# Norms of one group made in parts, and fetches asked for piece by piece, in a chunked delta rule with a maxout FFN behind it

## The chip, the cores and the metric

The kernel runs on one core of a Trainium2 chip. The core has five engines, each with a queue of its own that it works off in order: PE (TensorE, matmuls and transposes into PSUM), DVE (VectorE), ACT (ScalarE), POOL (GpSimd) and SP (SyncE, which here only issues DMAs). POOL and ACT issue DMAs too. The metric is the device time of one execution in microseconds, as the median of several runs.

## The reference

A delta rule over 4 batches x 8 heads, 768 tokens, head size 48; its output, 3072 tokens x 384, goes through a feed-forward net whose hidden value is the largest of three products:

```python
k_n = k / (np.linalg.norm(k, axis=-1, keepdims=True) + 1e-06)
for t in range(S):
    y[:, :, t] = einsum('bhd,bhde->bhe', q[:, :, t], state)
    v_old = einsum('bhde,bhd->bhe', state, k_n[:, :, t])
    state = state + beta[:, :, t] * outer(k_n[:, :, t], v[:, :, t] - v_old)
x = y.transpose(0, 2, 1, 3).reshape(B * S, H * D)        # 3072 x 384
h = maximum(maximum(x @ w1, x @ w2), x @ w3)             # 384 -> 768
out = h @ w_out                                          # 768 -> 384
```

q, k, v and beta are fp32. The four weight matrices come as 64-bit floats.

## The kernel before, in words

**The delta rule in chunks.** The 768 tokens are 12 chunks `c` of 64 tokens; two chunks make a group `m` (six groups, 512 tokens each over the four batches). Keys and queries are loaded in units `n` (two to a chunk). For a unit, `turn` (L329) puts keys and queries on the other axis by PE transposes, and `gram` (L411) makes the products of keys with keys and queries. The triangular systems of a whole group are solved on DVE by `solve(m)` (L514), a generator: it makes the key norms (`norm`, L275, one square root on ACT and five small DVE operations), turns them for the values (`norms_of`, L292, four DVE transposes), makes the scale (L539 to L549), scales the matrix once (L560) and then takes 31 elimination steps of two DVE operations each (L574 and L578). Each `yield` ends one part; `some(solving, n)` runs the next n parts.

**The recurrence.** Along the chunks run the links, each a function with a letter: `z` (`join_z`), `j` (`join_u`), `k` (`old_k`: keys times state on PE, L756, subtracted from the values on DVE, L768), `q` (`old_q`), `u` (`new`), `s` (`step`: a product on PE, L807, added to the state by DVE, L814), `y` (`to_y`, the sum on DVE in L828) and `x` (`to_x`, the transpose for the FFN). `e`, `f` and `d` (`halves_z`, `halves_u`, `turn_t1`) finish the solved blocks. Values are scaled with the norms on POOL (`scale`, L302).

**The FFN between which they stand.** `ffn(m)` (L1249) is a generator too: each yield ends one product of 128 hidden rows (`p_h`, L1261), which ACT copies out (L1269) or DVE joins by a maximum (L1275). In group 0 a product covers 256 tokens; a product is six matmul rows of the profile. The loop over `ffn(0)` (L1505) hands out the rest of the work between these pieces `i` by tables: `FIRST` (links of chunk 1, solve parts `S1`, query transposes `T4` to `T7`), `EARLY_LINKS`, `SOLVED` (further solve parts of group 1), `CONVERTED`, `FETCHED`, `LESS`. The schedule is written out by hand (`manual_schedule`): each engine and each DMA queue runs its instructions in the order in which this loop emits them.

**Weights.** There are 24 pieces of 128 x 384 numbers (0 to 17 of the three hidden matrices, 18 to 23 of the output matrix). `fetch` (L220) brings the next piece's 64-bit words into one of five buffers `w_bits` (384 KB). `weights` (L236) makes fp32 of it: three ACT operations (L255 to L257), and one part later, in `join_last`, a shift on DVE (L266) and an add on POOL (L270); `mant` and `up` between them have two buffers each. A buffer is free for the fetch five pieces later when the ACT operations have read it.

**Queues.** `load_q(n)` (L142) issues two DMAs into one of three query buffers and so waits for the transposes of unit n-3. `load_v(c)` (L145) issues two DMAs into one of three value buffers. `queries` (L1486) runs `load_q(n + 3)` behind each `T` n, on SP. Before the change, between the pieces of `ffn(0)`, SP's queue holds: weight 8, queries 4, 5, weight 9, queries 6, weight 10, values 2, weights 11 and 12, queries 7, weight 13, queries 8, 9, 10, values 3 and 4.

The group that the change calls second is `m == 1`. Its `solve` stands at the start of `ffn(0)`: its first part is run before the loop (L1417), then come 10 parts in pieces 0 to 3 (`S1` in `FIRST`) and the rest by `SOLVED`. Its work array `y_p` is one of the three large PSUM buffers (`two`), so that the links have two left until it is done.

Of the kernel before, what the change touches and what calls it, by code (L numbers as in the profile page):

```python
# [23 lines left out]
def kernel(  # L24
# [93 lines left out]
    def rows(bb):  # L118
        return slice(C * bb, C * (bb + 1))
# [6 lines left out]
    def load(src, dst, n, queues):  # L126
        c, g = divmod(n, 2)
        for bb in range(2):
            queues[bb].dma_start(
                out=dst[rows(bb ^ g), :, 0:D],  # L130
                in_=src[2 * bb + g, :, c * C : (c + 1) * C, :].rearrange(
                    "h p d -> p h d"
                ),
            )
# [7 lines left out]
    def load_q(n, queues=one_queue):  # L142
        load(q, qpad[n % NQ], n, queues)

    def load_v(c, queue=nc.sync):  # L145
        vts[c] = work.tile([128, 2, H, D], FP32, name="v_t", bufs=3)
        for bb in range(2):
            queue.dma_start(  # L148
                out=vts[c][rows(bb)].rearrange("p g h d -> p (g h) d"),
                in_=v[2 * bb : 2 * bb + 2, :, c * C : (c + 1) * C, :].rearrange(  # L150
                    "b h p d -> p (b h) d"
                ),
            )
# [132 lines left out]
    def small(name, *shape):  # L286
        one = name[-1] == "0" or name[-2:] == "bl" or name == "warm"
        return work.tile([128, *shape], FP32, name=name, bufs=2 - one)
# [3 lines left out]
    def norms_of(m, bl):  # L292
        for cc in range(2):
            t = small("nrm", 48)
            for bb in range(2):
                at = 16 * (1 - bb)
                nc.vector.transpose(
                    out=t[rows(bb), at : at + BL], in_=bl[rows(cc)]
                )
            nrms[2 * m + cc] = t[:, 16:32].rearrange("p (g h) -> p g h", g=2)  # L300

    def scale(c, nrm):  # L302
        (nc.vector if c > 9 else nc.gpsimd).tensor_tensor(
            out=vts[c], in0=vts[c],
            in1=nrm[:, :, :, None].to_broadcast([128, 2, H, D]), op=ALU.mult,
        )
# [207 lines left out]
    def solve(m):  # L514
# [15 lines left out]
        if m == 1:  # L530
            y = ps_two("y_p").rearrange("p b (j i) -> p (b j) i", i=BL)
            nc.scalar.copy(y, zero.to_broadcast(y.shape))
        if m == 2:
            yield
        if m:
            norms_of(m, bl)
            if m == 2:
                yield
            nc.vector.reciprocal(bl, bl)  # L539
        else:  # L540
            bl_0.append(bl)
            bl = small("inv_bl", BL)
            nc.vector.reciprocal(bl, bl_0[0])
# [11 lines left out]
        else:  # L555
            size, xv, yv = BL, x[:, None], y[:, None]
            xb, by = x, bl[:, None, :].to_broadcast([128, BL, BL])
        if m == 2:
            yield
        nc.vector.tensor_tensor(out=xb, in0=xb, in1=by, op=ALU.mult)  # L560
        yield
        for j in range(size - 1):
            a, b = j + 1, size - 1 - j
            n = BL // size
# [19 lines left out]
        if m == 0:  # L584
# [3 lines left out]
            for i in range(4):  # L588
                if i % 2:
                    n = H * (i == 3)  # L590
# [895 lines left out]
    def queries(names):  # L1486
# [9 lines left out]


    CONVERTED = {*range(6), *range(11, 17), 18, *range(21, 30)}
    FETCHED = {8: 1, 12: 1, 13: 1, 14: 1, 21: 2, 22: 1, 23: 1, 24: 1, 25: 1}
    LESS = {3: 0, 6: 1, 9: 2, 18: 3, 21: 4, 25: 5}  # L1500
    SOLVED = {
        **{i + 4: n for i, n in enumerate((3, 2, 2, 2, 3, 3, 3, 3, 2, 2))},
        27: 1, 28: 1, 29: 1, 30: 6, 31: 17, 32: 6, 33: 5,
    }
    for i, _ in enumerate(ffn(0)):  # L1505
        if i < 7:
            fetch(nc.sync if i else nc.gpsimd)
        if i == 0:
            scale(1, nrm_0[:, 1])
        if i == 1:  # L1510
            load_q(4)
            load_q(5)
        if i == 2:
            load_q(6)
        if i < 6:
            join_last()
        for _ in range(FETCHED.get(i, 0)):
            fetch(nc.gpsimd)
        queries(FIRST.get(i, ""))
        links(1, EARLY_LINKS.get(i, ""))  # L1520
        if i == 26:
            solving = solve(2)
            some(solving, 1)
        if i in CONVERTED:
            some(conv, 1)
        if i == 0:
            fetch(nc.gpsimd)
        some(solving, SOLVED.get(i, 0))
        if i in (8, 13):
            prep_values(i // 4)  # L1530
        if i in (4, 8):
            for n in range(2):
                load_k(8 + 2 * (i > 4) + n, (nc.gpsimd, nc.gpsimd))
        if i == 11:
            load_q(11, (nc.gpsimd, nc.gpsimd))
        if i in (3, 9, 10, 21):
            load_v((3, 9, 10, 21).index(i) + 2)
        if i == 18:
            blocks(2)
        if i == 30:  # L1540
            prep_values(4)
        if i in (29, 30, 31):
            load_blocks(i - 17, nc.sync)
        if i in LESS:
            less_first(LESS[i], nc.gpsimd if i < 10 else nc.vector)
        if i in (30, 31):
            turn_first((2 * i - 60, 2 * i - 59))
        if i == 31:
            turn_first((4, 5))
            for t in range(KT):  # L1550
                both_layers(t)
                if t == 0:
                    links(1, "x1")
# [53 lines left out]
```

## Time and profile before

| | |
|---|---|
| median of 3 runs | 503.69 us (503.05 to 505.37) |
| the profiled execution | 505.88 us |
| its span, first to last instruction | 504.2 us |
| mean granted TensorE clock | 0.969 |
| PE busy | 481.9 us, 96% |
| DVE busy | 354.8 us, 70% |
| ACT busy | 168.7 us, 33% |
| POOL busy | 189.8 us, 38% |
| DMA | 53.51 MB, 106 GB/s over the span |

The shares are means over stages that differ. The start (to some 45 us) is the first group's solve with little for PE to do. From 45 us on the FFN gives PE work between the links; the change lies between 45 and 90 us. From some 105 us to the end PE is hardly ever idle. An engine's row in the order of time gives the start, the length and, in brackets, how long the engine was idle ahead of it and what ended that; "issue" there means that it waited for nothing that the profile shows.

### The profile page before, as it was taken

What the parts mean: (1) busy time and instruction counts of PE and PEld (TensorE: products, weight loads), DVE (VectorE), ACT (ScalarE), POOL (GpSimd) and SP (SyncE); (2) the same over time, 40 slices, a digit from 0 to 9 for tenths busy, and PEclk for the clock granted to TensorE, in tenths of its full rate; (3) what the DMA queues carried; (4) which work ended last, traced back from release to release, by engine and by line L of the source; (5) the groups of instructions that cost most, each with busy time, mean ns of one, the idle gap of its engine ahead of it and who ended that gap; (6) DMA issues with size and microseconds to landing.
All of it is one profiled execution on the core that took longest, in us unless ns stands there. A gap on an engine that the chain in (4) does not pass through costs nothing.

```text
span 504.2 us, 18764 instructions
## 1 busy us (share of the span) xinstructions
PE 481.9 (96%) x8100; PEld 344.5 (68%) x8100; DVE 354.8 (70%) x830; ACT 168.7 (33%) x323; POOL 189.8 (38%) x313
## 2 busy tenths in 40 slices
PE   7679789999999999999999999999999999999997
PEld 6568578878765555665545665555698446998896
DVE  5888989757698362879552899565998874478763
ACT  5577655876321152210242210243110123113310
POOL 7426583764580294880483890511000020000000
PEclk9758899999999999999989999999999999999999
DMA  8937969775260664644674653654223330340001
GB/s 111 198 61 204 201 170 151 187 189 126 66 159 9 139 132 100 160 107 113 139 143 76 164 132 88 134 88 96 65 49 79 64 85 4 82 95 16 1 16 48
DMA packets 110114, 53.51 MB, mean 106 GB/s; under 512 B 93264, under 2 KB 103920, under 8 KB 110032
## 3 DMA queue, kind: packets, MB, share of 16 engines
q1 hardware_dynamic: 98528, 32.01, 32.0%
q0 software_dynamic: 9088, 19.72, 15.5%
q8 instruction: 64, 1.05, 0.9%
q10 hardware_dynamic: 2416, 0.59, 0.7%
q14 instruction: 18, 0.15, 0.1%
HBM read 39.17 MB, written 13.11 MB: 104 GB/s over the span
## 4 chain that ended last, share of the span: by engine, by line
PE 83%; DMA 5%; DVE 4%; ACT 2%; issue 2%; POOL 1%; SPq 1%; DVEq 0%; POOLq 0%; ACTq 0%
PE p_h L1261 30%; PE p_o L1304 13%; PE p_o L998 12%; PE p_c L1199 5%; PE p_g L422 4%; PE p_u L784 2%; PE p_m L918 2%; PE p_y L826 2%; PE p_k L756 2%; PE p_q L756 2%; PE p_j L739 2%; PE p_t L345 2%; PE p_s L807 2%; DMA qall<-in_q_dram 2%; PE p_z L726 1%
## 5 line engine op out<-in xcount | busy, mean ns | idle before, releaser
L1261 PE MATMUL p_h<-xt,w_sb 128*128 128x512 f32 (+1 forms) x468 | 179.6, 528 | 0.6 <-ACT xt L852 0.4
L1261 PEld LDWEIGHTS p_h<-xt,w_sb 128*128 128x128 f32 x468 | 85.9, 193 | 63.1 <-issue 54.2
L1275 DVE TENSOR_TENSOR h<-h,p_h 128x512 f32<-128x512 f32 (+1 forms) x42 | 23.9, 569 | 56.6 <-PE p_h L1261 54.0
L578 DVE TENSOR_TENSOR y_bl<-y_bl,tmp 128x31 f32<-128x31 f32 (+20 forms) x139 | 50.6, 364 | 4.8
L1304 PE MATMUL p_o<-wo_sb,h 128*128 128x384 f32 x144 | 49.2, 490 | 0.4 <-POOL wo_sb L270 0.4
L574 DVE TENSOR_TENSOR tmp<-x_bl,y_bl 128x31 f32<-128x31 f32 (+20 forms) x139 | 46.0, 331 | 4.1
L380 POOL DMA_DIRECT2D turned<-in_q_dram x72 | 39.1, 551 | 6.1 <-POOL turned L375 2.8
L1271 ACT ACTIVATE h<-p_h 128x512 f32<-128x512 f32 (+1 forms) x30 | 16.6, 552 | 72.6 <-PE p_h L1261 72.5
L1304 PEld LDWEIGHTS p_o<-wo_sb,h 128*128 128x128 f32 x144 | 26.8, 190 | 18.5 <-POOL wo_sb L270 1.0
L270 POOL TENSOR_TENSOR w_sb<-mant,up 128x384 int32<-128x384 int32 x18 | 18.8, 1045 | 33.6 <-DVE mant L266 28.6
L422 PEld LDWEIGHTS p_g<-kqt 48*64 48x64 f32 x1216 | 24.7, 143 | 9.7 <-issue 7.4
L422 PE MATMUL p_g<-kqt 48*64 48x64 f32 (+1 forms) x1216 | 28.0, 243 | 0.9 <-ACT kqt L351 0.8
L1310 ACT COPY o_sb<-p_o 128x384 f32<-128x384 f32 x12 | 5.8, 479 | 61.7 <-PE p_o L1304 54.4
L375 POOL MEMSET turned<- 128x96 f32 x18 | 3.3, 189 | 59.4 <-DVE kqt L396 59.4
L611 POOL DMA_DIRECT2D ut<-y_d x4 | 2.6, 650 | 60.4 <-DMA y_d<-y_bl 60.4
L148 POOL DMA_DIRECT2D v_t<-in_v_dram x14 | 11.5, 829 | 30.7 <-PE p_u L784 30.7
L814 DVE TENSOR_TENSOR st<-st,p_s 48x768 f32<-48x768 f32 (+1 forms) x18 | 17.1, 951 | 7.4 <-PE p_s L807 6.9
L406 DVE TENSOR_TENSOR pt<-p_g,mask 128x512 f32<-128x512 f32 x20 | 13.7, 690 | 10.4 <-PE p_g L422 10.3
L1304 PE MATMUL p_o<-w_sb,xt 128*128 128x384 f32 x60 | 21.0, 486 | 0.0
L768 DVE TENSOR_TENSOR v_t<-v_t,p_k 128x768 f32<-128x768 f32 x11 | 10.4, 950 | 13.1 <-PE p_k L756 13.1
L439 ACT COPY at<-p_g 128x512 f32<-128x512 f32 x22 | 12.7, 583 | 18.6 <-DVE pt L406 16.2
L784 PEld LDWEIGHTS p_u<-v_t,ut 64*64 64x64 f32 x768 | 13.7, 141 | 7.7 <-issue 7.7
(247 smaller groups left out, 917.8 us busy)
## 6 DMA issues: line engine op xcount, KB each, us to landing
w_bits<-in_moe_w_dram SPq DMA_DIRECT2D x9, 384.0 KB, 6.1
w_bits<-in_moe_w_dram POOLq DMA_DIRECT2D x9, 384.0 KB, 5.4
turned<-in_q_dram POOLq DMA_DIRECT2D x72, 48.0 KB, 2.6
out_dram<-o_sb SPq DMA_DIRECT2D x34, 96.0 KB, 2.3
y_x<-y SPq DMA_DIRECT2D x32, 96.0 KB, 2.3
qall<-y_x SPq DMA_DIRECT2D x32, 96.0 KB, 2.8
v_t<-in_v_dram POOLq DMA_DIRECT2D x14, 192.0 KB, 4.7
at_d<-at SPq DMA_DIRECT2D x76, 32.0 KB, 2.1
```

Source lines behind the costliest of these rows:

```text
L270: nc.gpsimd.tensor_tensor(out=dst.bitcast(I32), in0=mant_v.bitcast(I32), in1=up_v, op=ALU.add)
L380: (queue, nc.gpsimd)[i].dma_start(out=t[p0 : p0 + 32, bb, at : at + NP * 2 * D].rearrange("p (j x) -> p j x", j=NP), in_=(k, q)[i][2 * bb ...
L422: nc.tensor.matmul(p_g[rows(bb ^ (g * i)), par, c0 : c0 + C * (1 + whole)], kq[:, 0], kq if whole else kq[:, i],)
L574: nc.vector.tensor_tensor(out=t_v, in0=row.to_broadcast(t_v.shape), in1=column.to_broadcast(t_v.shape), op=ALU.mult,)
L578: nc.vector.tensor_tensor(out=rest, in0=rest, in1=t_v, op=ALU.subtract)
L756: nc.tensor.matmul(p_b[rows(bb), par, c0 : c0 + D], kqt[g][dims(par), j, bb ^ g, i], st[dims(par), bb ^ g, g, j],)
L784: nc.tensor.matmul(p_v[rows(bb ^ g), g, i], ut[c % NU][rows(bb), g, h], rhs[rows(bb), g, h],)
L998: nc.tensor.matmul(to[:, g], a[j][:, 128 * g : 128 * (g + 1)], b[j], start=(start and g == of[0] and j == 0), stop=(stop and g == of[-1] a ...
L1199: nc.tensor.matmul(to, w[stays], moves, start=(n == 0), stop=(n == len(terms) - 1))
L1261: nc.tensor.matmul(p_h, w_sb[i][:, t, f * 128 : (f + 1) * 128], xt[:, t, lo : lo + w], start=(t == 0), stop=(t == KT - 1),)
L1275: nc.vector.tensor_tensor(out=h, in0=h, in1=p_h, op=ALU.max)
L1304: nc.tensor.matmul(p_o, stays, moves, start=(n == 0), stop=(n == len(terms) - 1))
```

## The change

In `solve`, three yields that only group 2 had now hold for group 1 too: behind the square root and the clearing of `y_p`, behind `norms_of`, and ahead of the scaling of the matrix (L560). What was one part run ahead of the loop becomes four, of which three are run by the `S1` entries of pieces 0 and 1. `SOLVED` runs one part more in each of pieces 4, 5 and 6, so that by the end of piece 6 as many elimination steps are done as before.

In the loop, the fetches on SP stand at pieces 0, 1, 2 and 6 to 10, where they stood at 0 to 6; the fetch on POOL at piece 8 is gone. `load_q(4)`, `load_q(5)`, `load_q(6)` stand at pieces 2, 3 and 4 (before: 1, 1 and 2), and `load_v(2)` at piece 5 (before: 3), which is behind `T4` and its `load_q(7)`.

```diff
@@ solve(m)
         if m == 1:
             y = ps_two("y_p").rearrange("p b (j i) -> p (b j) i", i=BL)
             nc.scalar.copy(y, zero.to_broadcast(y.shape))
-        if m == 2:
+        if m in (1, 2):
             yield
         if m:
             norms_of(m, bl)
-            if m == 2:
+            if m in (1, 2):
                 yield
             nc.vector.reciprocal(bl, bl)
...
-        if m == 2:
+        if m in (1, 2):
             yield
         nc.vector.tensor_tensor(out=xb, in0=xb, in1=by, op=ALU.mult)
         yield
@@ tables and loop of ffn(0)
-    FETCHED = {8: 1, 12: 1, 13: 1, 14: 1, 21: 2, 22: 1, 23: 1, 24: 1, 25: 1}
+    FETCHED = {12: 1, 13: 1, 14: 1, 21: 2, 22: 1, 23: 1, 24: 1, 25: 1}
     SOLVED = {
-        **{i + 4: n for i, n in enumerate((3, 2, 2, 2, 3, 3, 3, 3, 2, 2))},
+        **{i + 4: n for i, n in enumerate((4, 3, 3, 2, 3, 3, 3, 3, 2, 2))},
         27: 1, 28: 1, 29: 1, 30: 6, 31: 17, 32: 6, 33: 5,
     }
     for i, _ in enumerate(ffn(0)):
-        if i < 7:
+        if i in (0, 1, 2, *range(6, 11)):
             fetch(nc.sync if i else nc.gpsimd)
         if i == 0:
             scale(1, nrm_0[:, 1])
-        if i == 1:
-            load_q(4)
-            load_q(5)
-        if i == 2:
-            load_q(6)
+        if i in (2, 3, 4):
+            load_q(i + 2)
...
-        if i in (3, 9, 10, 21):
-            load_v((3, 9, 10, 21).index(i) + 2)
+        if i in (5, 9, 10, 21):
+            load_v((5, 9, 10, 21).index(i) + 2)
```

## The prediction

> **What bounds the kernel now.** I read the page first: the slices, then the chain that ended last.
>
> ```profile
> span 504.2 us, 18764 instructions
> ...
> PE   7679789999999999999999999999999999999997
> ...
> DVE  5888989757698362879552899565998874478763
> ...
> PEclk9758899999999999999989999999999999999999
> ...
> PE 83%; DMA 5%; DVE 4%; ACT 2%; issue 2%; POOL 1%; SPq 1%; DVEq 0%; POOLq 0%; ACTq 0%
> ```
>
> PE ends the kernel: from the seventh slice on (76 us) it is never under 90%. What can be won lies before that, and the change touches only 45 to 90 us. There I asked for busy time by stretches (start:end, length, then busy time of PE, PE's weight load, DVE, ACT, POOL; granted clock; DMA share; GB/s).
>
> ```profile
> 50.00:55.00 5.00, 2.87 (x72) 2.27 (x72) 4.90 (x10) 1.02 (x3) 3.49 (x4) 1.00 1.11 202
> 55.00:60.00 5.00, 4.84 (x135) 3.70 (x135) 4.76 (x14) 3.83 (x10) 1.74 (x2) 0.66 1.06 237
> 60.00:65.00 5.00, 3.90 (x139) 3.08 (x135) 4.73 (x14) 3.71 (x7) 3.37 (x3) 1.00 0.95 186
> 65.00:70.00 5.00, 3.69 (x78) 3.04 (x77) 4.76 (x13) 3.19 (x7) 4.32 (x6) 1.00 0.48 135
> ```
>
> DVE is full (4.7 to 4.9 of 5) where PE has holes: DVE bounds this stage. Third, both engines in order of time:
>
> ```profile
> 48.13 0.86 DVE L297 STREAM_TRANSPOSE nrm<-bl 64x32 f32<-64x32 f32 x4
> ...
> 50.05 1.22 DVE L560 TENSOR_TENSOR wo_sb<-wo_sb,bl 128x1024 f32<-128x1024 f32 x1
> 51.18 1.63 DVE L266 TENSOR_SCALAR mant<-mant 128x384 uint32<-128x384 uint32 x1
> ...
> 54.16 0.95 DVE L814 TENSOR_TENSOR st<-st,p_s 128x768 f32<-128x768 f32 x1
> ...
> 72.23 0.95 DVE L828 TENSOR_TENSOR y<-qs,p_y 128x768 f32<-128x768 f32 x1 [1.65 <-PE p_y L826]
> ```
> ```profile
> 55.16 1.19 PE L756 MATMUL p_k<-st,kqt 48*64 48x48 f32 x64 [2.19 <-DVE st L814]
> 56.28 2.93 PE L1261 MATMUL p_h<-xt,w_sb 128*128 128x256 f32 x6
> ...
> 63.55 0.39 PE L739 MATMUL p_j<-z,t 32*32 32x32 f32 x23 [0.98 <-issue]
> ...
> 68.53 0.68 PE L784 MATMUL p_u<-v_t,ut 64*64 64x48 f32 x30 [1.31 <-issue]
> ```
> ```profile
> 51.12 1.47 POOL L303 TENSOR_TENSOR v_t<-v_t,nrm 128x768 f32<-128x768 f32 x1 [3.48 <-DMA v_t<-in_v_dram]
> 52.95 0.99 POOL L270 TENSOR_TENSOR w_sb<-mant,up 128x384 int32<-128x384 int32 x1 [0.36 <-DVE tmp L574]
> ```
> ```profile
> 47.21 4.13 SPq L129 DMA_DIRECT2D qall<-in_q_dram  x4
> 51.44 2.06 SPq L224 DMA_DIRECT2D w_bits<-in_moe_w_dram  x1
> ```
>
> See four things. PE idles 2.19 us until the state add L814 is done, and the next product takes 2.93 us instead of 1.5. Two more holes (0.98, 1.31) wait for no engine. Between 43 and 76 us DVE waits once, 1.65 us for `p_y`, which those holes make late. And the shift in L266 takes 1.63 us beside POOL's scaling, where the same shift elsewhere takes 0.35.
>
> **Part 1: the norms in parts.** Nothing is added; only DVE's order changes. Before, behind the norm (it ends at 48.1): turns, reciprocal to copy, scaling L560, shift (weight 3), two elimination steps, maximum L1275, shift (weight 4), state add. In the built order of the new kernel: shift (3), turns, reciprocal to copy, maximum, shift (4), state add, scaling, two steps, maximum. Steps from one start to the next, from the rows: 0.27 shift, 0.90 turns, 1.05 for four small operations, 0.33 maximum, 0.27 shift. The state add starts at 48.13 + 2.82 = 50.95, not 54.16. The 3.2 us are the scaling (1.13), two steps (0.83) and the shift's collision with POOL (1.55 - 0.27 = 1.28). Its result at 51.9 is ahead of PE, which is at `p_f` until 52.97: the 2.19 us hole goes.
>
> Followed on: scaling, two steps, maximum to 54.16; shift (5); L768 and the mask to 56.1; two steps; shift (6); the `d` transposes end at 58.99 (before 62.05). PE gets through `p_u` some 4 us earlier, `p_y` at 67.1 instead of 72.2.
>
> **Where that gain goes.** Three parts are added to pieces 4 to 6, so by the maximum that started at 75.90 DVE has done the same 17 elimination steps. It can be earlier only by what DVE loses: 1.65 us idle before L828, 0.14 before the next state add, 1.28 of collision, 3.1 us in all. PE's 4 us end in waits for DVE: `T5` needs the PSUM buffer that L828 empties, later products wait for their maximum. Up to 85 us DVE then waits just 0.34 us, so its gain is the stage's gain.
>
> Of the 3.1 us the idle 1.79 go, as DVE would reach L828 at about 68.7, behind `p_y`. The collision is open: in the new order the second shift ends at 50.95, and POOL starts L303 at 51.12 when values 1 have landed. 0.17 us decide; I take half, 0.64. Ends: 0 and 1.28.
>
> **Part 2: weight 9 ahead of queries 4 to 6.** Its buffer is free at 48.6 (ACT has read weight 4); SP gets to it then instead of at 51.44. The queries' four DMAs occupied SP for 4.13 us and go behind: 49.2 to 55.3 for all six. They are needed by `T4`, `T5`, `T6` (69.13, 73.25, 75.7 before); no cost, with 9 us of cover. What pays is values 1 on POOL's queue, issued at 44.27, awaited by L303 until 51.12: weight 9's 384 KB now fly beside them. Behind L303 stand POOL's add of weight 3, ACT's operations for weight 5 (53.98; ACT waited 4.28 us for that add), DVE's shift of it. This shift comes at 54.16 in the new order and ACT's result at 54.1: no slack, a us late there is a us lost. From below: -0.4 is possible, as four small query DMAs leave the place. From above: 2.1 us, the time that weight 9 took SP's queue at 51.44. I take 0.3: w_bits landed in 3.7 to 7.3 us, so the bulk of weight 9 flies behind 51 us.
>
> **Part 3: weights 10 to 14, values 2.** SP held weights 10, 11, 12 and values 2 from 55.7 to 63.5 and now sends them behind `T4`. SP's new order: queries 7 (1.7 us, after `T4` at some 64.5), values 2 (2.4), weight 10 (0.6), queries 8 (2.0), and so on to values 4 at about 82; before, 85. The weights are used from piece 11 on (86.8 before, some 84 after); weight 10 goes out at 69: hidden by 10 us or more. Values 2 leave at 66.4 to 68.8 instead of 56.3; v_t DMAs here took 4.6 to 7.5 us, so landed by 73.4 to 76.3, plus 1.47 on POOL. L768 of chunk 2, at 80.72 before, would come at 78.0: slack 0.2 to 3.1 us, cost 0. Behind this scale on POOL's queue wait keys 10 and 11 (2.8 us of issue; kpad landed in 4.7): issued by 79, landed by 84 to 87, needed by the transposes at 89.55 before, 86 to 87 after. The fetch that POOL gives up at piece 8 returns 0.76 us.
>
> The holes at 62.6 and 67.2 stand where the DMA share is 0.95 and 0.48; with weights 11 and 12 gone from there they may close. Worth 0 to 2.3 us to PE, and 0 to the sum, since PE is ahead of DVE there.
>
> **Sum.** 1.79 + 0.64 - 0.3 = 2.1 us at 85 us. Behind it ACT is full (5.00 of 5 us from 90 to 95) with conversions that start when DVE is through; they move with it. At 103.61 PE waits 0.26 us for such a weight, so a PE further ahead would wait there. From there the chain is PE's and carries the gain to the end. Span 504.2 - 2.1 = 502.1; the profiled execution, 505.88 with 1.7 around its span, would be 503.8; it stood 2.2 over the median, so by the median 503.69 - 2.1 = **501.6**.
>
> **The clock, weighed.** PE's clock was 0.50 from 57 to 59 us, behind the hole of 2.19 us, and `p_h` took 2.93 instead of 1.5 us. The Trainium skill, page "TensorE: Matmul & The Clock Gate", Part 1, has the clock halved after a mostly idle window of about 3.4 us that runs freely; by it 1.4 us come back too, and with them the sum would be 500.2. With that rule the trace's one drop there agrees. The same rule speaks against the change where a new hole opens (third rival).
>
> **Rivals.**
> *PE sets the gain (13%).* If DVE's order leaves it slack that I don't see (the collision gone, its rows faster without POOL beside them), the gain is the hole and the slow product, 2.19 + 1.4 = 3.6: 500.1. Against it: DVE at 4.76 of 5.
> *Values 1 late behind weight 9 (20%).* Both DMA queues are busy at 50 us (share 1.11). With the full 2.1 us late, DVE's shift waits as long: 1.79 + 1.28 - 2.1 = 1.0: 502.7. The skill's "DMA: Bandwidth & Descriptors", section on queues, rings and completion order, has each DMA engine take turns between queues by packet, which speaks for this one; no run here shows the turns.
> *A new hole halves the clock (9%).* PE would be done with the state product at 68.1 and wait until 69.7 for L828. A hole of 1.31 us left the clock at 1.00, one of 2.19 did not; 1.6 is between. Cost up to 1.4, of which PE's lead over DVE (0.7 us) hides half: 502.3.
> *Values 2 late: slower (13%).* It decides when they land beyond 76.5: from there each us holds up POOL, L768 and DVE's queue behind it, maximum and all. At 78.6 the gain is gone (503.7); at 82, 5.5 us late, 507.1. For it: 4.6 MB are asked for in some 18 us, 256 GB/s, and the fullest 5 us stretch here moved 251. Against: only keys 8, 9 and queries 7 are ahead of them.
> *No difference (5%).* The catch-up in pieces 4 to 6 gives all back: 503.7.
>
> **Numbers.** The forecast has 40%, from 501.0 to 502.4. The range goes from 500.0 (PE sets the gain) to 505.2 (values 2 land at 80) and leaves out some 15%. Half a per cent, 2.5 us, is about what a measurement here tells from no change. Faster by that (under 501.2): 13% and a third of the forecast's cases, and some of the clock's, 28%. Slower (over 506.2): the far half of values 2 and what I haven't seen, 11%. The rest, 61%.
>
> **What would show it.** Right: `p_k` follows `p_f` with under 0.3 us of idle; L814 starts near 51; `y_p`'s last step ends some 2 us before 88.2; L828 without idle before it. Wrong: L303 after 51.5; POOL waiting at the second L303 past 76 us; a clock of 0.5 between 65 and 80 us; a wait for `kpad` or `v_t` on PE or DVE near 80.

## The result, and the profile after

The changed kernel is slower: 510.56 us median of 6 runs (508.32 to 513.96), where the kernel before had 502.97 (502.22 to 505.37, 6 runs). The ratio is 1.0155, with a 95% interval of 1.0111 to 1.0199. The forecast was 501.6 us, with a range up to 505.2 and a chance of 11% for slower. The profiled execution took 510.76 us. In this document medians are of all runs, while the ratios leave out runs that lie over 1.5% above the fastest of the same kernel, which takes away part of the upper heap where runs lie in two heaps.

The page of the changed kernel, span and chain that ended last. DMA, SP's queue ("SPq") and "issue" have grown to 8, 3 and 3% from 5, 1 and 2%:

```profile
span 509.1 us, 18766 instructions
...
PE 79%; DMA 8%; DVE 4%; SPq 3%; issue 3%; ACT 2%; POOL 0%; POOLq 0%; DVEq 0%; ACTq 0%
```

First the stage that the prediction worked on, DVE and then PE of the changed kernel in order of time (start, length, engine, line, what; in brackets the idle time ahead and what ended it):

```profile
47.02 0.18 DVE L282 TENSOR_SCALAR bl<-nt_bl 128x32 f32<-128x32 f32 x1
...
50.58 0.95 DVE L814 TENSOR_TENSOR st<-st,p_s 128x768 f32<-128x768 f32 x1 [0.69 <-PE p_s L807]
51.45 1.50 DVE L560 TENSOR_TENSOR wo_sb<-wo_sb,bl 128x1024 f32<-128x1024 f32 x1
...
54.44 1.38 DVE L266 TENSOR_SCALAR mant<-mant 128x384 uint32<-128x384 uint32 x1 [0.20 <-ACT mant L255]
56.48 0.95 DVE L768 TENSOR_TENSOR v_t<-v_t,p_k 128x768 f32<-128x768 f32 x1 [0.67 <-PE p_k L756]
...
70.44 0.94 DVE L828 TENSOR_TENSOR y<-qs,p_y 128x768 f32<-128x768 f32 x1
...
86.88 0.20 DVE L578 TENSOR_TENSOR y_p<-y_p,tmp 128x31 f32<-128x31 f32 x1
```
```profile
50.23 0.31 PE L807 MATMUL p_s<-u,kpad 64*64 64x48 f32 x2 [0.87 <-issue]
...
52.92 1.01 PE L756 MATMUL p_k<-st,kqt 48*64 48x48 f32 x55
56.08 0.37 PE L756 MATMUL p_k<-st,kqt 48*64 48x48 f32 x9 [2.14 <-issue]
...
71.44 0.66 PE L345 MATMUL p_t<-ident,qall 128*128 128x128 f32 x4 [1.63 <-DVE y L828]
```

The state add starts at 50.58 (before 54.16), L828 comes without idle at 70.44 (72.23), the last elimination step starts at 86.88 (88.00). The old hole of 2.19 us ahead of `p_k` is gone, but two new ones stand at `p_s` and inside `p_k`, 0.87 and 2.14 us, and wait for no engine. Up to 100 us the kernel is still ahead. It loses behind that.

Of this lead 0.9 us is older than the change. The last row of the norm, up to which both kernels run the same, is this one in the kernel before, at 47.91 instead of 47.02 us:

```profile
47.91 0.18 DVE L282 TENSOR_SCALAR bl<-nt_bl 128x32 f32<-128x32 f32 x1
```

The difference was there at 33 us (L318 at 34.09 and 33.17). In the twenty profiles of this document L318 starts anywhere from 32.9 to 36.3 us, so times of two profiles are best compared by their distance from such a row.

PE of the changed kernel from 102 us:

```profile
102.12 1.56 PE L1261 MATMUL p_h<-xt,w_sb 128*128 128x256 f32 x6 [0.51 <-POOL w_sb L270]
104.70 0.25 PE L726 MATMUL p_z<-ut,at 32*32 32x32 f32 x4 [1.01 <-DMA ut<-y_d]
105.28 0.72 PE L726 MATMUL p_z<-ut,at 32*32 32x32 f32 x60 [0.33 <-DMA ut<-y_d]
109.09 0.32 PE L726 MATMUL p_z<-ut,at 32*32 32x32 f32 x4 [3.09 <-DMA ut<-y_d]
110.58 1.07 PE L726 MATMUL p_z<-ut,at 32*32 32x32 f32 x60 [1.18 <-DMA ut<-y_d]
111.58 4.43 PE L1261 MATMUL p_h<-xt,w_sb 128*128 128x256 f32 x12
115.94 0.75 PE L739 MATMUL p_j<-z,t 32*32 32x32 f32 x64
```

The same stretch of the kernel before:

```profile
103.61 1.56 PE L1261 MATMUL p_h<-xt,w_sb 128*128 128x256 f32 x6 [0.26 <-POOL w_sb L270]
105.11 1.35 PE L726 MATMUL p_z<-ut,at 32*32 32x32 f32 x128
106.39 2.86 PE L1261 MATMUL p_h<-xt,w_sb 128*128 128x256 f32 x12
109.17 0.75 PE L739 MATMUL p_j<-z,t 32*32 32x32 f32 x64
```

`p_z` of the second group needs `ut`, the solved blocks that SP writes to device memory (`y_d`, L599) and reads back (L611). It now waits for them four times, 5.6 us in all, its own rows take 2.36 us instead of 1.35, and the granted clock is 0.5 for 6.8 us, from 108.0 us on while PE still waits, so that the next twelve rows of `p_h` take 4.43 instead of 2.86 us. With the lead of 1.5 us at 102 us this is -1.5 + 5.6 + 1.0 + 1.6 = 6.7 us; the `p_j` behind starts 6.8 us later. The first `p_o` stands at 135.0 instead of 128.7, and from there to the end the changed kernel takes 374.1 us, the kernel before 375.5. These two executions end 4.9 us apart, the medians 7.6: the profiled execution of the kernel before (505.88 us) was one of its longer ones.

SP's queue, first of the changed kernel, then of the kernel before (here the length of a row is how long SP was occupied with asking):

```profile
79.69 4.65 SPq L148 DMA_DIRECT2D v_t<-in_v_dram  x2
84.43 3.65 SPq L224 DMA_DIRECT2D w_bits<-in_moe_w_dram  x1
88.27 1.31 SPq L148 DMA_DIRECT2D v_t<-in_v_dram  x2
89.68 6.02 SPq L452 DMA_DIRECT2D at_d<-at  x4
95.80 1.16 SPq L599 DMA_DIRECT2D y_d<-wo_sb  x2
101.31 4.03 SPq L611 DMA_DIRECT2D ut<-y_d  x8
```
```profile
80.12 4.99 SPq L148 DMA_DIRECT2D v_t<-in_v_dram  x4
90.50 1.80 SPq L452 DMA_DIRECT2D at_d<-at  x4
92.40 1.15 SPq L599 DMA_DIRECT2D y_d<-wo_sb  x2
96.53 4.94 SPq L611 DMA_DIRECT2D ut<-y_d  x8
```

SP was free from 85.1 to 90.5 in the kernel before. In the changed kernel it stands in its own asking almost without a break from 79.7 to 97: one weight fetch takes it 3.65 us instead of some 0.6, and four small writes of `at_d`, 1.80 us before, take 6.02. `y_d`, whose source is ready earlier than before (the elimination ends sooner), is asked 3.4 us later and its reads begin 4.8 us later. The stretches suggest why the asking is slow (changed kernel; the last two columns are DMA share and GB/s):

```profile
60.00:65.00 5.00, 5.00 (x156) 4.03 (x158) 4.73 (x14) 4.79 (x9) 3.80 (x4) 0.98 0.01 3
...
85.00:90.00 5.00, 5.00 (x54) 3.89 (x52) 3.94 (x14) 3.21 (x7) 3.95 (x5) 1.00 1.08 145
90.00:95.00 5.00, 4.97 (x115) 4.28 (x115) 3.91 (x5) 5.00 (x11) 3.97 (x5) 1.00 1.22 231
```

From 60 to 65 us the DMA engines now stand empty (0.01; before 0.95), and from 85 to 95 they are over full (1.08 and 1.22; before 0.70 and 0.75).

### The profile page after: what moved, and what is told of

Read it like the earlier page. It is cut to its first block, busy times and chain, and to the rows that moved or that the text cites. A ratio compares the mean times of both kernels' runs of the same rounds, so it can differ in the third digit from the quotient of the medians.

```text
span 509.1 us, 18766 instructions
## 1 busy us (share of the span) xinstructions
PE 483.4 (95%) x8100; PEld 345.8 (68%) x8100; DVE 356.5 (70%) x830; ACT 168.3 (33%) x323; POOL 190.0 (37%) x312
## 3 DMA queue, kind: packets, MB, share of 16 engines
q8 instruction: 64, 1.05, 0.9%
## 4 chain that ended last, share of the span: by engine, by line
PE 79%; DMA 8%; DVE 4%; SPq 3%; issue 3%; ACT 2%; POOL 0%; POOLq 0%; DVEq 0%; ACTq 0%
PE p_h L1261 30%; PE p_o L1304 12%; PE p_o L998 10%; PE p_c L1199 4%; PE p_g L422 3%; PE p_y L826 2%; PE p_u L784 2%; PE p_m L918 2%; PE p_k L756 2%; DMA kmore<-in_k_dram 2%; DMA v_t<-in_v_dram 2%; PE p_s L807 2%; PE p_q L756 2%; PE p_j L739 2%; SPq L129 1%
## 5 line engine op out<-in xcount | busy, mean ns | idle before, releaser
L574 DVE TENSOR_TENSOR tmp<-x_bl,y_bl 128x31 f32<-128x31 f32 (+20 forms) x139 | 48.3, 347 | 4.1
L611 POOL DMA_DIRECT2D ut<-y_d x4 | 2.6, 652 | 60.3 <-DMA y_d<-y_bl 60.3
L768 DVE TENSOR_TENSOR v_t<-v_t,p_k 128x768 f32<-128x768 f32 x11 | 10.4, 950 | 13.4 <-PE p_k L756 13.3
L730 ACT COPY z<-p_z 32x512 f32<-32x512 f32 (+1 forms) x26 | 14.1, 543 | 14.7 <-PE p_z L726 14.2
```

The lines of the kernel that those rows point to most:

```text
L574: nc.vector.tensor_tensor(out=t_v, in0=row.to_broadcast(t_v.shape), in1=column.to_broadcast(t_v.shape), op=ALU.mult,)
```

## The experiments

Eighteen kernels, each beside the kernel before on the same chip. The three columns on the right are from each kernel's profile, one execution: how long from the first to the fourth asking of `at_d`, when the first read of `ut` is asked, and PE's idle at `p_z` for `ut`.

| kernel | median us (before) | ratio, 95% interval | `at_d` | `ut` | `p_z` |
|---|---|---|---|---|---|
| changed kernel | 510.56 (502.97) | 1.0155 [1.0111, 1.0199] | 5.6 | 101.3 | 5.6 |
| norms only | 506.64 (504.06) | 1.0031 [0.9990, 1.0072] | 1.4 | 99.0 | 0 |
| fetches only | 512.98 (504.06) | 1.0172 [1.0115, 1.0228] | 5.8 | 103.0 | 5.6 |
| weight 14 on POOL | 511.96 (504.06) | 1.0150 [1.0081, 1.0219] | 5.0 | 103.0 | 5.4 |
| weights 10 to 14 on POOL | 510.65 (504.06) | 1.0083 [1.0033, 1.0132] | 1.8 | 99.4 | 0 |
| weights back | 503.84 (503.61) | 1.0002 [0.9977, 1.0027] | 1.4 | 96.6 | 0 |
| weights only | 512.15 (503.61) | 1.0133 [1.0076, 1.0190] | 4.8 | 101.8 | 5.1 |
| values 4 late | 506.43 (503.61) | 1.0041 [1.0014, 1.0068] | 1.3 | 98.4 | 0 |
| weights 10 to 12 in the gap | 503.68 (503.61) | 1.0000 [0.9976, 1.0024] | 1.3 | 95.2 | 0 |
| extra reads on SP | 505.30 (504.15) | 1.0011 [0.9964, 1.0059] | 1.3 | 97.0 | 0 |
| extra reads on POOL | 507.40 (504.15) | 1.0032 [0.9980, 1.0083] | 1.3 | 98.9 | 0 |
| gap and values 4 late | 507.90 (504.15) | 1.0089 [1.0054, 1.0124] | 1.3 | 97.7 | 0 |
| `y_d` on ACT | 509.49 (504.25) | 1.0066 [1.0016, 1.0117] | 4.4 | 96.0 | 0 |
| large pile ahead of `at_d` | 504.15 (504.25) | 1.0008 [0.9971, 1.0045] | 1.3 | 98.7 | 0 |
| the same two reads at pieces 3 and 4 | 505.43 (504.25) | 1.0046 [1.0017, 1.0076] | 1.3 | 95.2 | 0 |
| small pile ahead of `at_d` | 504.91 (503.02) | 1.0032 [1.0002, 1.0063] | 2.8 | 98.3 | 0 |
| `p_z` later, changed kernel | 512.61 (503.02) | 1.0174 [1.0103, 1.0245] | 4.7 | 103.3 | 0 |
| `p_z` later, kernel before | 510.56 (503.02) | 1.0118 [1.0049, 1.0187] | 1.3 | 94.0 | 0 |

Not in the table is the kernel with more matmuls ahead, a single run of 509.91 us, told last.

**Which part.** First the two parts alone.

Norms only: the kernel before with the three yields and `SOLVED` of the changed one.

```diff
-        if m == 2:
+        if m in (1, 2):
             yield
-        **{i + 4: n for i, n in enumerate((3, 2, 2, 2, 3, 3, 3, 3, 2, 2))},
+        **{i + 4: n for i, n in enumerate((4, 3, 3, 2, 3, 3, 3, 3, 2, 2))},
```

> The kernel before with part 1 alone: the three yields in the solve and 4, 3, 3 in SOLVED; every fetch stands where it stood. Theory A (the queue): the loss of the changed kernel comes from SP's queue, in which weights 10 to 14 now stand between the queries and values 3 and 4, so that the writes of unit 8 and of the solved blocks y_d leave late; part 1 has no share in it. The product p_h of piece 16 then starts 1 to 2 us earlier than in the kernel before, nothing takes that back, and the time is 0.3 to 0.6% shorter: 500 to 502. Theory C (the norms): the catch-up of three solve parts is what makes it late; then this kernel is slower by 3 us or more. Theory B (the bytes) says the same as A here.

Measured 506.64 us, ratio 1.0031: no gain that can be told, and not the 500 to 502 expected. Its profile, of a long execution (511.03 us), shows what became of the forecast gain, PE and then DVE:

```profile
53.24 0.31 PE L807 MATMUL p_s<-u,kpad 64*64 64x48 f32 x2 [0.87 <-issue]
...
59.08 0.46 PE L756 MATMUL p_k<-st,kqt 48*64 48x48 f32 x9 [2.14 <-issue]
```
```profile
54.46 1.97 DVE L560 TENSOR_TENSOR wo_sb<-wo_sb,bl 128x1024 f32<-128x1024 f32 x1
57.91 1.40 DVE L266 TENSOR_SCALAR mant<-mant 128x384 uint32<-128x384 uint32 x1 [0.19 <-ACT mant L255]
```

The same two holes as in the changed kernel, to the hundredth, and the collision of DVE with POOL has moved: the scaling L560 takes 1.97 us (before 1.22; in the changed kernel 1.50), a later shift 1.40 (1.38).

Fetches only: the changed kernel without those lines.

```diff
-        if m in (1, 2):
+        if m == 2:
             yield
-        **{i + 4: n for i, n in enumerate((4, 3, 3, 2, 3, 3, 3, 3, 2, 2))},
+        **{i + 4: n for i, n in enumerate((3, 2, 2, 2, 3, 3, 3, 3, 2, 2))},
```

> The changed kernel without part 1: solve and SOLVED as before, all fetches moved. Theory A and theory B: as slow as the changed kernel or up to 2 us slower, 510 to 513, y_d written some 3 us later than in the kernel before (92.4), ut read some 5 us later (96.5). Theory C: the time of the kernel before, 502 to 504.

512.98 us, the whole loss, with the same wait of 5.6 us at `p_z`. So it lies in the fetches. Which of them is told by four kernels.

Weights back (changed kernel, weight fetches as before, so that norms, queries 4 to 6 and values 2 stay changed):

```diff
-    FETCHED = {12: 1, 13: 1, 14: 1, 21: 2, 22: 1, 23: 1, 24: 1, 25: 1}
+    FETCHED = {8: 1, 12: 1, 13: 1, 14: 1, 21: 2, 22: 1, 23: 1, 24: 1, 25: 1}
-        if i in (0, 1, 2, *range(6, 11)):
+        if i < 7:
```

> The changed kernel with the weights' fetches where the kernel before has them (pieces 0 to 6 on SP, weight 14 on POOL at piece 8); queries 4 to 6 and values 2 stay moved, part 1 stays. Theory A (SP's queue is held by the late weights) and theory B (their bytes fill the DMA engines between 65 and 95 us, whoever asks): no wait of p_z for ut, 503 to 506. Rival D (values 2 behind queries 7 are what shifts everything on SP): as slow as the changed kernel, 509 to 512.

Weights only (kernel before with these two lines turned the other way):

```diff
-    FETCHED = {8: 1, 12: 1, 13: 1, 14: 1, 21: 2, 22: 1, 23: 1, 24: 1, 25: 1}
+    FETCHED = {12: 1, 13: 1, 14: 1, 21: 2, 22: 1, 23: 1, 24: 1, 25: 1}
-        if i < 7:
+        if i in (0, 1, 2, *range(6, 11)):
```

> The kernel before with the weights' fetches moved alone (pieces 0, 1, 2, 6 to 10, weight 14 on SP); queries, values 2 and the solve as before. Theories A and B: slow, p_z waits 3 us or more for ut, 508 to 512; the part short of the changed kernel is what values 2 (384 KB less in the crowd) are worth. Rival D: 503 to 505.

Weights 10 to 12 in the gap (changed kernel; 13 and 14 stay late on SP):

```diff
-        if i in (0, 1, 2, *range(6, 11)):
+        if i in (0, 1, 2, 3, 4, 5, 9, 10):
```

> The changed kernel with weights 10, 11 and 12 asked for at pieces 3, 4 and 5, into the stretch from 57 to 65 us in which its DMA engines stand idle (share 0.40 and 0.01), and only weights 13 and 14 at 9 and 10, on SP as before. Theory B: 1.15 MB less between 65 and 95 us, the wait of p_z gone or under 1 us, 503 to 506. Theory A in its narrow form (the fetch right ahead of values 4 and the writes holds SP): weights 13 and 14 still stand there, 509 or more.

Values 4 late (changed kernel):

```diff
-        if i in (5, 9, 10, 21):
-            load_v((5, 9, 10, 21).index(i) + 2)
+        if i in (5, 9, 20, 21):
+            load_v((5, 9, 20, 21).index(i) + 2)
```

> The changed kernel with values 4 asked for at piece 20 and not at piece 10 (their scaling comes at piece 30): 384 KB leave the crowd ahead of unit 8's and y_d's writes and SP has two DMAs less to send before them. Theories A and B: the read of ut starts some 2 to 4 us earlier than 101.3 after the same start, p_z waits that much less, 506 to 508. If the write of y_d is late for another reason (the solve itself): no change, 510 or more.

With the weights back the loss is gone (503.84 beside 503.61), with the weights alone it is all there (512.15). Put into the gap where the DMA engines stand empty, weights 10 to 12 cost nothing (503.68). So the move of weights 10 to 14 makes the kernel slow, and it takes the move of 10, 11 and 12, from 56 to 63 us to 70 to 77 us: weights 13 and 14 late do no harm without it. Whether 10 to 12 late would be enough without 13 and 14 was not tested. SP's queue with the weights alone:

```profile
89.54 5.26 SPq L452 DMA_DIRECT2D at_d<-at  x4
94.90 2.71 SPq L599 DMA_DIRECT2D y_d<-wo_sb  x2
101.79 4.04 SPq L611 DMA_DIRECT2D ut<-y_d  x8
```

It is the changed kernel's picture again, and `p_z` waits 5.1 us for `ut`. With values 4 out of the way the reads of `ut` begin at 98.4, `p_z` does not wait, and most of the loss is gone (ratio 1.0041), but the kernel stays 2.8 us behind. Both out of the way together:

```diff
-        if i in (0, 1, 2, *range(6, 11)):
+        if i in (0, 1, 2, 3, 4, 5, 9, 10):
...
-        if i in (5, 9, 10, 21):
-            load_v((5, 9, 10, 21).index(i) + 2)
+        if i in (5, 9, 20, 21):
+            load_v((5, 9, 20, 21).index(i) + 2)
```

> Weights 10, 11 and 12 in the gap at pieces 3, 4 and 5, 13 and 14 at pieces 9 and 10, and values 4 asked at piece 20; the rest as in the changed kernel. If the pile ahead of at_d and ut is all that was left: 502 to 504 us, ut at 94 to 96, p_z without a wait. If values 4 are not what is in the way any more: as the kernel with weights 10 to 12 in the gap, 503.7.

That was missed: 507.90, slower than with the gap alone. `p_z` does not wait, and the clock is halved at 121 us instead. PE's longest idle from 95 to 140 us is a hole of 1.69 us at 120.3 that waits for no engine, of the kind told last. Late values 4 seem to have a price of their own; of which wait it is made I did not test.

**Why a late weight is dear: asking, or bytes?** Theory A has it that SP's time in asking is the cost, B that the bytes fill the DMA engines, whoever asks.

Weight 14 back on POOL (changed kernel):

```diff
-    FETCHED = {12: 1, 13: 1, 14: 1, 21: 2, 22: 1, 23: 1, 24: 1, 25: 1}
+    FETCHED = {8: 1, 12: 1, 13: 1, 14: 1, 21: 2, 22: 1, 23: 1, 24: 1, 25: 1}
-        if i in (0, 1, 2, *range(6, 11)):
+        if i in (0, 1, 2, *range(6, 10)):
```

> The changed kernel with one fetch put back: weight 14 on POOL at piece 8, where the kernel before has it, and not on SP at piece 10. Theory A: that fetch held SP for 3.65 us between values 3 and values 4, so the read of ut starts 2 to 4 us earlier than the 101.3 us of the changed kernel, and the time falls by as much: 506 to 508. Theory B (the DMA engines are full of the same bytes, whoever asks): 509.5 or more, as the bytes and nearly their time stay.

Weights 10 to 14 asked by POOL (changed kernel):

```diff
-            fetch(nc.sync if i else nc.gpsimd)
+            fetch(nc.sync if 0 < i < 6 else nc.gpsimd)
```

> The changed kernel with weights 10 to 14 asked for at the same pieces, 6 to 10, by POOL and not by SP. Bytes and pieces stay. Theory A: SP is through with values 4 at 82 to 84 us, the writes of unit 8 take some 2 us and not 6, y_d leaves by 92, and the gain of part 1 shows: 500 to 503. Theory B: the time of the changed kernel, 509 or more.

Weight 14 was not it: without it on SP's queue, values 3 and 4 take SP 9.03 us instead, and the loss stays (511.96). With all five on POOL the median is still 510.65, in runs from 504.8 to 515.5; the profiled one, at 505.0, has no wait at `p_z`. SP was not through with values 4 at 82 to 84, as A expected, but at 90.5. SP's queue of the two:

```profile
83.39 9.03 SPq L148 DMA_DIRECT2D v_t<-in_v_dram  x4
92.52 5.44 SPq L452 DMA_DIRECT2D at_d<-at  x4
```
```profile
79.83 10.69 SPq L148 DMA_DIRECT2D v_t<-in_v_dram  x4
90.71 2.24 SPq L452 DMA_DIRECT2D at_d<-at  x4
```

This spoke for the bytes. So I put bytes alone into the kernel before. These kernels add reads whose numbers nothing uses; what they compute is unchanged.

```diff
+        if i in (7, 8, 9):
+            nc.sync.dma_start(
+                out=w_sb[i - 7][:, :, 512:768].bitcast(U32), in_=pieces[i][1]
+            )
```

> The kernel before, with three more reads of 384 KB on SP's queue at pieces 7, 8 and 9 (into columns of the weight words' tiles that nothing reads; the numbers are not used): the bytes that the moved weights 10 to 12 add there, while the weights themselves stand where they stood. If bytes or queue time between 65 and 95 us are the cause (theories A and B): 508 to 512 us, SP's at_d writes lengthened beyond 4 us, the first ut read after 99 us, p_z with waits for ut. If the cause is that the weights themselves come late for what is made of them: 503 to 505 us, ut at 96 to 98.

The same with `nc.gpsimd.dma_start`:

> The same three reads as in the run with them on SP, asked by POOL's queue at the same pieces. Theory B (bytes, whoever asks): as slow as on SP, 506 to 512 us, ut after 98. Theory A (SP's time in asking): 503 to 505 us, ut at 96 to 97.

On SP the reads missed what A and B both expected: 505.30 us. On POOL the median, 507.40, lies where B expected it (nine runs from 502.8 to 512.0, one at 1655.8). Both ratios hold 1. Three of ten runs with the reads on SP did stand at 511.7 to 512.4, the place of the changed kernel, the other seven at 505.5 or less. So B as I had put it, late bytes cost by themselves, does not hold for most of the runs. Nor is a high DMA share enough: with the reads on SP it is 1.18, 1.01 and 1.12 in the three stretches from 80 to 95 us (changed kernel 1.21, 1.08, 1.22), and `at_d` is asked in 1.80 us as before. The DMA groups between 64 and 92 us (count, size, median us from asking to landing) show a difference at nearly the same number of 384 KB fetches (7 with the weights moved, 6 with the extra reads); kernel before, weights only, extra reads on SP:

```profile
v_t<-in_v_dram SPq DMA_DIRECT2D x4, 192.0 KB, 5.0
```
```profile
v_t<-in_v_dram SPq DMA_DIRECT2D x4, 192.0 KB, 7.9
```
```profile
v_t<-in_v_dram SPq DMA_DIRECT2D x4, 192.0 KB, 6.4
```

With the extra reads values land in 6.4 us, with the moved weights in 7.9; SP is through with values 4 at 88.3 and `at_d` is asked at 90.45. Is the pile enough? Two reads of 384 KB right ahead of `at_d` (kernel before; a second kernel has one such read at each of pieces 3 and 4, some 25 us earlier):

```diff
+        if i in (10,):
+            for n in range(2):
+                spare = dram.tile([128, KT, 256], U32, name="spare")
+                nc.sync.dma_start(out=spare, in_=pieces[n][1])
```

> The kernel before, with two more reads of 384 KB on SP's queue at piece 10, right behind values 4 and ahead of unit 8's at_d (from the weight words into device memory that nothing reads). Theory F (what is unserved on SP's queue when at_d is asked): at_d's four writes take 4 us and more instead of 1.8, ut's reads begin after 99 us, p_z waits for ut, 508 to 513 us. If the weights' own lateness is the cause instead: no wait of p_z, 503 to 505 us.

> The kernel before with the same two reads of 384 KB on SP's queue, one at piece 3 and one at piece 4, where the DMA engines stand empty from about 62 to 70 us. Theory F: they are through before 70, at_d's writes take 1.8 us, ut at 96 to 98, 503 to 506 us, though as many bytes are moved in the stage as in the run with the pile ahead of at_d. Theory B in its first form (bytes of the stage): as slow as that run.

Neither decides: 504.15 and 505.43. The reads ahead of `at_d` were asked from 87.2 to 88.9 and landed 5.2 to 5.3 us later, at 92.5 and 93.5, so that little of them was left when `at_d` came at 92.35 (1.79 us for its four writes). The early two were asked at 58.75 and 62.48, where the kernel before has no empty stretch (a DMA share of 0.95 from 60 to 65 us). In small packets instead, four reads of values:

```diff
+        if i == 10:
+            for c in (3, 4):
+                spare = dram.tile([128, 2 * H, D], FP32, name="spare")
+                for bb in range(2):
+                    nc.sync.dma_start(
+                        out=spare[rows(bb)],
+                        in_=v[2 * bb : 2 * bb + 2, :, c * C : (c + 1) * C, :].rearrange(
+                            "b h p d -> p (b h) d"
+                        ),
+                    )
```

> The kernel before with four more reads of 192 KB each, of values in the small packets of L148, into device memory that nothing reads, on SP's queue at piece 10 behind values 4 and ahead of unit 8's at_d. The theory that a pile on SP's queue at 89.5 us is enough (F): at_d's writes take 4 us or more, ut from 100 us on, p_z waits, 508 to 514 us. If not: 503 to 505.

504.91, ratio 1.0032. These reads bring 4,160 packets more than the page of the kernel before has, the two large reads 800, for the same 0.79 MB. `at_d` took 3.27 us and the reads of `ut` began at 98.3: half a pile, and `p_z` did not wait.

The landings tell how large the pile is. When `at_d` is asked, the last read ahead of it on SP's queue still has 7.9 us to go in the changed kernel (values 4, asked at 88.92 and landed at 97.6), and 6.7 to 10.0 us in all six kernels whose `at_d` takes over 4 us in the table. In the others, as far as the landings are in the trace, it is 3.7 us or less: 1.1 with the large pile, 2.9 with the extra reads on SP. Of the small pile the last landing is missing; the read before it had 3.2 us to go. So my added reads did not make the pile of the changed kernel.

All profiles together show a step. Where the first read of `ut` is asked 6.6 us or more before PE is ready for `p_z`, PE waits for none of them; in the four kernels where it is 0.3 to 3.4 us and `p_z` stands in its place, PE waits 5.1 to 5.6 us. With my added reads it was never under 6.7.

**The order in SP's queue.** The changed kernel with the writes of `y_d` asked by ACT, past the pile:

```diff
-            nc.sync.dma_start(
+            (nc.scalar if m == 1 else nc.sync).dma_start(
                 out=y_d[cc].rearrange("f b h i j -> (f b h) i j"),
```

> The changed kernel with one edit: the two writes of y_d of the second group are asked by ACT's queue instead of SP's, where they stand behind four writes of at_d and what is unserved of the fetches. The same bytes at nearly the same time. If the order in SP's queue is the cause (theory F): y_d is asked near 91 us instead of 95.8, ut's reads begin at 95 to 98 instead of 101.3, p_z waits less than 1 us or not at all, the clock stays, and the time is 501 to 505 us. If the load of the DMA engines is (theory B): y_d lands as late as before, ut at 99 to 101, 508 to 512 us.

The profile does what was expected of the queue's order. SP's asking is as slow as in the changed kernel, but `y_d` leaves at 89.28 and `p_z` does not wait; SP, ACT's queue and PE:

```profile
90.56 4.93 SPq L452 DMA_DIRECT2D at_d<-at  x4
95.98 6.34 SPq L611 DMA_DIRECT2D ut<-y_d  x8
```
```profile
89.28 0.51 ACTq L599 DMA_DIRECT2D y_d<-wo_sb  x1
```
```profile
103.93 1.35 PE L726 MATMUL p_z<-ut,at 32*32 32x32 f32 x128
```

That execution took 503.36 us. But the ten runs lie in two heaps, four from 503.4 to 507.7 and six from 508.8 to 513.5, with a median of 509.49. What the six lose, no profile shows, as none of them was profiled: `ut`'s last read is still asked at 101.8, close to its need at 104.5, so it may be the old wait; it may be something else.

**The wait itself.** The changed kernel, and as a control the kernel before, with `p_z` four pieces later:

```diff
-        16: "g2", 17: "g3", 20: "d0 d1 z0 z1", 22: "j0", 24: "j1 u0", 26: "s0",
+        16: "g2", 17: "g3", 24: "d0 d1 z0 z1", 25: "j0", 26: "j1 u0", 27: "s0",
```

> The changed kernel with the links of the second group that read ut (the transposes of d, p_z) at piece 24 instead of 20, and p_j, the first p_u and the first p_s one piece apart behind them (25, 26, 27); all fetches as in the changed kernel. If the wait for ut with the halved clock behind it is the loss (theory G): p_z without idle, clock 1.0 from 105 to 120, and 502 to 506 us, as the control. If the fetches cost it elsewhere (instruction fetches, the DMA load): 508 to 513 us with no wait at p_z.

> The kernel before with the same later p_z, the control of the run above: 503 to 506 us; more, if the shorter distance of the links behind piece 24 costs something itself.

Inconclusive: the control itself is slow (510.56), so the later place has a price of its own, and 512.61 beside it says little. The wait for `ut` is gone in the changed kernel's profile, which took 516.08 us all the same, and holes of the other kind stand there instead:

```profile
113.72 0.37 PE L726 MATMUL p_z<-ut,at 32*32 32x32 f32 x19 [1.10 <-issue]
...
123.86 0.34 PE L784 MATMUL p_u<-v_t,ut 64*64 64x48 f32 x2 [3.62 <-issue]
```

**What the "issue" holes are.** Counted through all matmul rows, the two holes of the kernel before stand ahead of rows 1231 and 1358, 127 apart. The kernel before with 20 more rows ahead of everything:

```diff
-    busy(6, ident)
+    busy(16, ident)
```

> The kernel before with 16 instead of 6 matmuls of the warming up at L1351, which adds 10 matmuls (20 instructions of PE with their weight loads) ahead of everything. If the holes of the elimination and the norms that have no waiting cause ('issue') stand at every 128th matmul, where new instructions are fetched, they move ahead by 10 matmuls or 20 rows in the sequence (with the holes now after 41 of p_j and 34 of p_u, to other places in them); if they belong to a transfer or a collision at that time, they stay at their time and place in the work. Time 503 to 506 us.

```profile
52.41 0.56 PE L807 MATMUL p_s<-u,kpad 64*64 64x48 f32 x22 [0.78 <-issue]
...
61.88 1.09 PE L756 MATMUL p_k<-st,kqt 48*64 48x48 f32 x29 [3.84 <-issue]
```

They show up at `p_s` after 42 rows of 64 and at `p_k` after 35, ahead of rows 978 and 1105, again 127 apart (a few rows can be missing from a trace). In the changed kernel, with 20 rows less ahead, they stood after 62 and after 55. So the place is a row number, not a piece of work or a moment. In all twenty profiles every hole of more than 0.5 us on PE that waits for nothing stands ahead of one of nine such rows, about 127 or a multiple of it apart, give or take a few (978, 1105, 1231, 1358, 1862, 2114, 2366, 2622 and 4659); with a few rows missing from the traces, that fits every 128th. Not as expected, other ones of these places had the stall than in the kernel before, and the holes at `p_j` and `p_u` were gone: the place is fixed, whether it stalls is not. The 3.84 us halved the clock for 6.8 us; this run took 509.91.

## Why the prediction was wrong

**Part 1** had the mechanism right and the gain wrong. Forecast was the state add at 50.95 (measured 50.58), L828 without idle (so it is), the elimination's end 2 us earlier (1.1), a piece of `p_h` at 102 us earlier by as much (1.5). But 0.9 us of these leads are older than the change. From the end of the norm (L282) to the last elimination step DVE took 39.86 us (47.02 to 86.88), before 40.09 (47.91 to 88.00): the terms 1.79 + 0.64 of the sum measured 0.2 us. Norms alone gave a ratio of 1.0031, at best 0.9990, or 0.5 us. The idle 1.79 us did go, but DVE now waits 0.69 us for `p_s`, 0.20 for `mant` and 0.67 for `p_k`, 1.56 in all: the hole of 2.19 us on PE was not lost time that comes back, two holes at every 128th row took its place, 0.87 + 2.14. And the collision of 1.28 us, taken at half, did not go away; L560 takes 1.50 us instead of 1.22 and another shift 1.38 instead of 0.35, 1.3 us together. One pair of profiles could hardly have shown such a gain: from L282 to the copy behind the last step (L582) DVE takes 38.2 to 42.7 us in the profiles with the old order and 39.1 to 41.7 with the new.

**Part 2** was near enough. Weight 9 ahead of the queries was to cost 0.3 us through values 1. From POOL's asking for them (43.36, before 44.27) to its L303 (50.40, before 51.12) it took 7.04 us instead of 6.85, so the cost is 0.2. The rival that has values 1 up to 2.1 us late falls.

**Part 3 is the step that failed.** It said "no cost", weights "hidden by 10 us or more", SP through with values 4 at about 82. The weights were in time for their use; no engine waits for their landing. What was wrong is SP: it was through at 89.6, with values 4 still 7.9 us from landing. I had added up askings of 0.6 us for a weight and some 2 for values, as rows of an uncrowded queue have them; in the crowd one weight took 3.65 and one value asking 3.99. And I followed only the moved fetches to their users. Behind values 4 on the same queue stand `at_d`, `y_d` and `ut`, and a wait of PE from 104 us on, some 15 us past the stage that I looked at; it is the 5.6 us that the sum lacks, with 2.6 more for slower rows at the halved clock. "From there the chain is PE's and carries the gain to the end" was the sentence that hid it.

**The rivals.** "Values 2 late" had the right danger, 256 GB/s asked where the fullest stretch had moved 251, and put it on the wrong DMA: values 2 were on POOL at 75.17 and L768 ran at 79.60 without a stall. Had I asked who comes last in the pile, the answer was `ut`. "A new hole halves the clock" named a place at L828: the hole came, 1.63 us ahead of 71.44, and the clock stayed at 1.00, so its price was nothing. The halving came at `p_z`: the clock fell at 108.0 us, behind 3.4 us in which PE was busy for 0.97. The Trainium skill, page "TensorE: Matmul & The Clock Gate", Part 1, has it halve after an idle window of about 3.4 us, with windows that run freely. The hole of 1.63 us agrees with that. But the stretch ahead of 108.0 was not idle throughout, and the holes of 2.19 us (kernel before) and 2.14 us halved the clock too (0.66 and 0.68 from 55 to 60 us): in these traces a window that was idle for the larger part was enough.

**What is shown and what is not.** Shown: the weights moved behind 70 us make the loss, alone and in full, and with 10 to 12 in the gap it is gone. Shown in four profiles: PE waits 5.1 to 5.6 us for `ut`, and the clock is halved with it. Shown by `y_d` on ACT: its place on SP's queue is what delays it. Not shown: that this wait is all of it. Without it in the profile, the kernels with the weights on POOL and with `y_d` on ACT still have most of their runs at 508 and more; whether PE waits in those runs is not known, as the profiled ones took 505.0 and 503.4. Nor could reads added to the kernel before make the same pile. So why moved weights leave 7 to 10 us unserved ahead of `at_d`, and added reads of the same size 3, stays open; that the empty gap from 60 to 66 us starts the crowd later is what the traces suggest, not what a run has settled. No version tried here beats the kernel before.

## What to carry to other kernels

When a fetch is moved later on a queue, follow everything that stands behind it on that queue, not only the one who needs it: the first late victim here was a small write and read-back 20 us and three DMAs further on. Price an asking by rows from a crowded stretch, and look at whether the move empties a stretch of the DMA engines (0.95 to 0.01) to fill one that is needed (0.75 to 1.22). And a hole that a stage closes is won only if the next limit of that engine is known; here the holes at fixed rows of its instruction stream stood right behind.

## What the runs showed of the hardware

*Holes at every 128th matmul row.* In dense stretches of small matmuls PE stops for up to 3.8 us at fixed row numbers; which of them stall differs from kernel to kernel. Each matmul has a weight load, so 128 rows are 256 instructions; the page of the profile lists an instruction queue of 64 packets and 1.05 MB, 16 KB each, and PE's 16,200 instructions make 63 blocks of 256. That the stop is the fetch of the next block fits all this, but no run changed the fetch itself. The Trainium skill, page "Runtime: NRT & Kernel Launch", section "Instruction fetch mechanics", has blocks of 16 KiB or 256 instructions, and the cost of crossing one "mostly hidden"; the block agrees with the row numbers here, the hiding does not hold where 64 matmuls take about 1 us.

*Asking can take long in a crowd.* A fetch that occupies SP for some 0.6 us elsewhere took it 3.65 (weight 14) and 3.99 us (one of values 3) at DMA shares over 1, and the first write of `at_d` (32 KB) 3.72 instead of 0.31. It is not the share alone: weight 11, asked at 74.08 in a stretch with a share of 1.16, took 0.57. The landing of values 3 and 4 went from 5.0 us (kernel before) to 7.9 (weights only).

*Large and small packets ahead of a write.* 768 KB copied within device memory in 800 packets landed 5.2 to 5.3 us after their asking, and the four writes behind them took SP 1.79 us as without them; 768 KB of values in 4,160 packets took up to 6.2 us, and the same writes 3.27 us. The large reads had 3.5 us between their asking and these writes, the small ones 0.1, so the size of the packets is not the only difference.
